# Routing 24 blocks as 6, 6, 4, 4, 4 instead of 6, 6, 5, 4, 3 in a fused attention and mixture-of-experts kernel

## The chip, the cores and the metric

The kernel runs on one core of a Trainium2 chip. The metric is device time in microseconds (us), the median of several runs. TensorE multiplies matrices, ScalarE evaluates functions and copies, VectorE and GpSimd do elementwise work, and SyncE issues most of the transfers. In the profile they are PE (PEld is TensorE's weight load), ACT, DVE, POOL and SP. An engine works through its own instructions in the order in which they are written, and waits at an instruction until what it needs from other engines has been signalled.

## The reference, cut to what matters

```
scores = scale * q @ k.T - slope_h * distance        # 4 x 8 heads, 768 tokens, head size 64
keep   = 8 global keys, and the 96 latest keys       # a window
x      = softmax(scores) @ v                         # as 3072 tokens x 512
noisy  = x @ w_gate + log1p(exp(x @ w_noise)) * noise
top2, weights = the two largest of 8 experts, softmax over the two
out[token] += weight * relu(x[token] @ w1[e]) @ w2[e]   # w1 512 x 1024, w2 1024 x 512
```

All of it is in float32. Each of the 3072 tokens goes to two of eight experts, so an expert gets about 768 tokens.

## The kernel before, in words

The 3072 tokens are 24 blocks of 128. **Attention** runs over 48 passes, two to a block, four heads to a pass (the loop variable `n` goes up by 2; the text calls n/2 the pass, from 0 to 47). In a pass VectorE makes the scores with their bias and row minimum for the next pass (`score`, L862), ScalarE takes the exponential (L865), TensorE transposes the probabilities of this pass (`trans`, L878), multiplies queries and keys for the pass after the next (`product`, L848) and probabilities with values for the pass before (`attend`, L899), and VectorE divides (`norm`, L910 to L915). `product` writes the two PSUM banks that `score` of the same pass has read, so it comes after it, and the next `score` comes after `product`. A `trans` group (L878, six transposes, four in the first block of a sequence) opens each pass on TensorE, so its start times are the passes' start times.

**The gate** of a block runs four blocks' worth of passes later, with block g in passes 2g+4 and 2g+5. `gate_t` transposes the block (L380) and copies it to SBUF (L389); `gate_l` multiplies by the gate's weights (L410) for two blocks of a routing at once, or for one where a routing's last block has no partner; `gate_s` adds up the parts (L423, L426) in the second of the two passes. `gate_l` also stores the block in DRAM: in `xd` for all blocks, in `xe` too for the blocks of the first three routings.

**Routing** turns logits into a table of which token sits at which place of which expert. It is done for a segment of blocks at a time (`SEG`), as a Python generator `route(r)` that emits one or a few instructions at each step. For a segment of w blocks it emits two ScalarE operations, some 15 small VectorE operations for log1p(exp), the top two per block (L502, L504), the weights (L527 to L539), running counts as small matmuls (L552, L554), five more small operations (L561 to L593), then for each block two masks (`mask`, L579) and one product with the masks' partner (`marks`, L603), and a group of matmuls (L628, two per block) that adds this to the table `tab` (L632). In routings 0 and 1 the blocks are marked three to a group with the masks on GpSimd. Routing 2 (`CLOSE`) has one group; where no earlier routing is still marking when it computes `row` (L585), the masks of all but two blocks go to GpSimd at once, and those two to VectorE one by one; otherwise all its masks go to GpSimd later, after L593. Routings 3 and 4 mark in groups of three, with the masks on VectorE. When routing 2 is done, GpSimd gathers the 512 first tokens of expert 0 from `xe`, and TensorE transposes them at the end of attention. Expert 0's first layer can then start on them while routings 3 and 4 are still under way.

Steps are dealt by hand-written rules. A routing starts in the pass after whose `gate_s` its last block is complete. `tick(place)` is called at seven places of a pass (0 to 3 after the four scores, 4 to 6 inside `norm`) and takes one step of one routing, routing 2 first; `finish` at the end of a pass takes three steps of routings 0 and 1 and five of the later ones. A step that yields `True` lets nothing more of that routing happen until place 4 of the next pass; one that yields 2 waits for `finish`. In the kernel before, routing 2 begins in pass 37 and routing 3 in pass 45.

**Expert 0's first layer** (`up(0, f)`, L1132) is eight units of 12 matmuls with 512 columns. After each third matmul a function `ahead` takes one of 32 entries of the table `slots`, which says how far routing 3 (`late`), routing 4 (`last`), the gate of the last block and the splitting of `w2` may go there. After each unit ScalarE takes the positive part (L1113, `hh`) and VectorE the rest that rounding left (L1117, `hl`). Splitting `w2` into a high and a low part is one ScalarE copy (L196) and one VectorE subtraction (L197) for each of eight slices. When all is done, `rank` (L301 to L315) sorts the experts by their token counts, and GpSimd gathers the other tokens. The second layer of expert 0 (`down`, L1169) follows on TensorE, and then the other seven experts, with up to 812 tokens for an expert (`CAPS`). More tokens than that would run a slow path under `tc.If` at the end.

SBUF tiles named `xg` rotate through seven buffers; `marks`, the gathers and `rank` take them in turn.

Of the kernel before, what the change touches and what calls it, by code (L numbers as in the profile page):

```python
# [10 lines left out]
F32 = mybir.dt.float32  # L11
# [10 lines left out]
P = 128  # L22
# [13 lines left out]
def tile_local_global_attention_then_moe(  # L36
# [14 lines left out]
    B, _, _, D, _, HP, Q = q.shape  # L51
    H = 2 * HP
    Dm = H * D
# [3 lines left out]
    E, _, F = w1.shape  # L57
    KC, FC = Dm // P, F // P
    NG = kT.shape[2] // NB - P
    N = B * S  # L60
    NT = B * NB
# [1 line left out]
    windowed = 1 <= n_local <= NP + 1 and 0 <= n_global <= NG  # L63
    scale = 1.0 / math.sqrt(D)
    slopes = [2.0 ** (-8.0 * (h + 1) / H) for h in range(H)]
    SEG = [(0, 6), (6, 12), (12, 17), (17, 21), (21, NT)]
    CLOSE = 2
    SW = max(z - a for a, z in SEG)

# [5 lines left out]
    gp = wctx.enter_context(tc.tile_pool(name="gp", bufs=1))  # L75
# [134 lines left out]
    xg, xt, xw = {}, {}, {}  # L210
# [163 lines left out]
    def gate_t(g):  # L374
        x = rowed[g] = XR.pop(g).rearrange("p h d -> p (h d)")
        stored[g] = gp.tile([P, 2 * Dm], U16, name="xt", bufs=4)
        halved(planes(stored[g]), words(x))
        ps = bank("m").rearrange("p (k t) -> p k t", k=KC)
        for k in range(KC):
            nc.tensor.transpose(ps[:, k], x[:, k * P:(k + 1) * P], ident)  # L380
        j = partner(g)
        if j is None:
            XT[g] = ys[2].rearrange("p (k t) -> p k t", k=KC)
            to = XT[g]
        else:
            if j == 0:
                XT[g + 1] = pairs[0].rearrange("p (k j t) -> p k j t", k=KC, j=2)
            to = XT[g + 1 - j][:, :, j]
        nc.scalar.activation(to, ps, AF.Copy)  # L389

    def store(g):
# [2 lines left out]
    def gate_l(g, later=None):  # L394
# [8 lines left out]
            return  # L403
        ps = bank("m")[:, :P]
        x = XT.pop(g)
        x = [x] if j is None else [x[:, :, i] for i in range(2)]
        for i, y in enumerate(x):
            c = 2 * E * (1 - i)
            for k in range(KC):
# [243 lines left out]
    with ExitStack() as actx:  # L653
# [142 lines left out]

        END, WAIT = 7, 8

        def begin():
            for x, _ in active:  # L800
                x.ready = {WAIT: 4, WAIT + 1: 6}.get(x.ready, 0)

        def go(y):
            x = y[0]
            v = next(x, 0)
            if v == 0:
                active.remove(y)
            elif v is True:
                x.ready = WAIT
            elif v == 2:  # L810
                x.ready = END
            elif v == LAST:
                x.ready = WAIT + 1

        def tick(place):
            for y in sorted(active, key=lambda y: y[1] != CLOSE):
                if y[0].ready <= place:
                    return go(y)

        def finish():  # L820
            for y in active[:]:
                n = 5 if y[1] >= CLOSE else 3
                while n and y in active and y[0].ready <= END:
                    go(y)
                    n -= 1

# [259 lines left out]
    with ExitStack() as mctx:  # L1086
# [118 lines left out]
        def back(e, i):  # L1205
# [11 lines left out]

        late, last = pending
        slots = {
            0: [(late, 24)], 1: [(gate_s, 2), (late, 27)], 2: [(gate_t, 1), (late, 30)], 3: [(late, 33)],  # L1220
            4: [(gate_l, 1), (late, 36)], 5: [(late, 39)], 6: [(gate_s, 1), (late, 42)], 7: [(late, 45), (last, 2)],
            8: [], 9: [(late, 48), (last, 5)], 10: [(last, 7)], 11: [(last, 8)],
            12: [(late, 52), (last, 9)], 13: [(last, 12)], 14: [(last, 14)], 15: [(late, 54), (last, 16)],
            16: [(last, 19)], 17: [(last, 21)], 18: [(last, 23)], 19: [(last, 26)],
            20: [(last, 30)], 21: [(last, 33)], 22: [(late, 57), (last, 35)], 23: [(last, 37)],
            24: [(last, 39)], 25: [(last, 42)], 26: [(late, 61)], 27: [(last, 45)],
            28: [(last, 48)], 29: [(late, 99), split], 30: [split], 31: [(last, 52)],
        }
        slot, parts = [0], [0]

# [392 lines left out]
```

## Time and profile before

| | |
|---|---|
| runs | 700.07, 835.5 and 700.47 us, median 700.47 |
| the profiled execution | 701.94 us |
| its span, first to last instruction | 700.2 us |
| mean granted TensorE clock | 0.999 |
| TensorE matmuls busy | 683.6 us, 98% |
| TensorE weight loads busy | 615.1 us, 88% |
| VectorE, ScalarE, GpSimd busy | 66%, 60%, 46% |

Attention fills the span from 0 to about 155.7 us, expert 0's first layer 155.7 to 181.1 us, and the experts the rest. Rows of the trace read as: engine, line of the kernel, operation, what is written and from what, shapes, and how many instructions were merged into the row. A time in brackets is how long the engine sat idle before it, and after the arrow stands what ended that. The profiled execution lies 1.74 us above its span and 1.47 us above the median of the runs.

### The profile page before, as it was taken

The page shows a single profiled execution, that of the slowest core. Times are in us where ns is not written, and L with a number is a line of the kernel's source. Part 1 is how long each engine was busy: PE and PEld are TensorE (multiplying, and loading weights), DVE is VectorE, ACT ScalarE, POOL GpSimd, SP SyncE. Part 2 cuts the span into 40 slices and gives each one's busy share as a digit, 9 for nine tenths or more (in the row PEclk, how much of TensorE's full clock was granted, in tenths as well). Part 3 has the DMA queues.
Part 4 walks back from the last instruction along what each step waited for, and adds up shares of the span by engine and source line. Part 5 has one row for each costly group of instructions (what it writes and reads, how often), then busy time and mean ns, then how long its engine had stood idle before and what let it go on. Part 6 is the DMA issues. An engine that isn't in the chain of part 4 may idle for free. (4 is left out here: it accounts for less than half of the span.)

```text
span 700.2 us, 16023 instructions
## 1 busy us (share of the span) xinstructions
PE 683.6 (98%) x5701; PEld 615.1 (88%) x5701; DVE 459.8 (66%) x1412; ACT 423.6 (60%) x912; POOL 324.5 (46%) x408
## 2 busy tenths in 40 slices
PE   6999999999999999999999999999999999999995
PEld 5888888888889889999999998999899899889984
DVE  7668788968928477656766676667377756757600
ACT  6888787762346576547755755486558647755510
POOL 3352837450288663264536444642645354541222
PEclk9999999999999999999999999999999999999999
DMA  8999978859394877257935884496459457842233
GB/s 249 328 306 313 277 230 282 296 168 359 116 259 91 163 181 158 49 122 136 218 60 122 166 174 75 125 168 148 82 151 249 63 136 163 184 74 91 32 47 49
DMA packets 132889, 116.61 MB, mean 167 GB/s; under 512 B 51866, under 2 KB 97050, under 8 KB 132800
## 3 DMA queue, kind: packets, MB, share of 16 engines
q1 hardware_dynamic: 121392, 89.35, 46.5%
q0 software_dynamic: 11264, 25.89, 20.3%
q8 instruction: 47, 0.77, 0.5%
q14 instruction: 42, 0.34, 0.1%
q10 hardware_dynamic: 144, 0.26, 0.1%
HBM read 71.07 MB, written 33.10 MB: 149 GB/s over the span
## 5 line engine op out<-in xcount | busy, mean ns | idle before, releaser
L1426 PE MATMUL bank<-xh,wall 128*128 128x384 f32 (+4 forms) x784 | 216.9, 342 | 1.0 <-ACT aside L1468 0.6
L1426 PEld LDWEIGHTS bank<-xh,wall 128*128 128x128 f32 x784 | 143.9, 188 | 5.4 <-ACT aside L1468 1.3
L1426 PE MATMUL bank<-xl,wall 128*128 128x384 f32 (+4 forms) x392 | 133.4, 340 | 0.0
L1145 POOL DMA_INDIRECT out_dram<-y,ids x40 | 64.7, 1617 | 124.8 <-ACT y L1142 121.0
L1169 PE MATMUL av<-w2h,hh 128*128 128x512 f32 x304 | 119.8, 394 | 1.5 <-ACT aside L1201 1.1
L197 DVE TENSOR_TENSOR wall<-raw,wall 128x512 fp32r<-128x512 f32 (+1 forms) x84 | 76.5, 918 | 66.3 <-ACT wall L196 66.2
L1169 PE MATMUL av<-w2h,hl 128*128 128x512 f32 x304 | 119.1, 392 | 0.0
L1169 PE MATMUL av<-w2l,hh 128*128 128x512 f32 x304 | 119.1, 392 | 0.0
L196 ACT ACTIVATE wall<-raw 128x512 fp32r<-128x512 f32 (+1 forms) x84 | 58.0, 698 | 47.5 <-POOL raw L1279 47.5
L1117 DVE SCALAR_TENSOR_TENSOR hl<-bank,hh 128x384 fp32r<-128x384 f32 (+4 forms) x84 | 47.1, 561 | 52.8 <-ACT hh L1113 51.8
L1426 PEld LDWEIGHTS bank<-xl,wall 128*128 128x128 f32 x392 | 73.9, 188 | 2.8
L865 ACT ACTIVATE a<-ns,mx 128x168 f32<-128x168 f32 (+1 forms) x192 | 67.8, 422 | 13.5 <-DVE mx L862 13.0
L251 POOL DMA_INDIRECT xg<-xd,ids x49 | 51.9, 1060 | 41.7 <-DVE place L302 29.8
L1169 PEld LDWEIGHTS av<-w2h,hl 128*128 128x128 f32 x304 | 57.1, 188 | 12.6
L862 DVE CUSTOM_DVE_ANT_0 ns<-sc,bias 128x168 f32<-128x168 f32 (+1 forms) x188 | 51.8, 320 | 24.3 <-PE sc L848 8.7
L1169 PEld LDWEIGHTS av<-w2h,hh 128*128 128x128 f32 x304 | 57.1, 188 | 11.0 <-ACT aside L1201 1.3
L1113 ACT ACTIVATE hh<-bank 128x384 fp32r<-128x384 f32 (+4 forms) x84 | 41.9, 498 | 39.2 <-DVE bank L1500 25.5
L1169 PEld LDWEIGHTS av<-w2l,hh 128*128 128x128 f32 x304 | 57.1, 188 | 9.4 <-DVE w2l L197 0.3
L1278 POOL TENSOR_TENSOR raw<-raw 128x256 f32<-128x256 f32 x28 | 22.1, 790 | 77.3 <-DVE wall L197 76.7
L899 PE MATMUL av<-vs,at 128*64 128x65 f32 (+1 forms) x768 | 57.3, 224 | 0.3 <-issue 0.3
L236 POOL COPY xt<-y 128x256 uint16<-128x256 uint16 x96 | 35.0, 401 | 46.7 <-DVE y L915 46.7
L899 PEld LDWEIGHTS av<-vs,at 128*64 128x64 f32 (+1 forms) x768 | 50.8, 136 | 2.4 <-issue 2.0
(219 smaller groups left out, 1465.5 us busy)
## 6 DMA issues: line engine op xcount, KB each, us to landing
raw<-in_w SPq DMA_DIRECT2D x64, 256.0 KB
raw<-in_w SPq DMA_DIRECT2D x32, 512.0 KB
out_dram<-zero SPq DMA_DIRECT2D x14, 512.0 KB
vs<-in_v SPq DMA_DIRECT2D x24, 260.0 KB
xd<-xt SPq DMA_DIRECT2D x24, 256.0 KB
qbuf<-in_q SPq DMA_DIRECT2D x23, 256.0 KB
ks<-in_k SPq DMA_DIRECT2D x20, 272.0 KB
xe<-y SPq DMA_DIRECT2D x17, 256.0 KB
```

What stands on the lines that cost most here:

```text
L196: nc.scalar.activation(hi, src, AF.Copy)
L197: eng.tensor_sub(lo, src, hi.bitcast(F32))
L236: nc.gpsimd.tensor_copy(to[:, :, c], frm[:, :, c])
L251: nc.gpsimd.indirect_dma_start(out=xg[e, t].bitcast(U16)[:m], out_offset=None, in_=xd[:n], in_offset=bass.IndirectOffsetOnAxis(ap=r, axis= ...
L862: nc.vector.tensor_tensor_reduce(out=ns[x][:, s, :w], in0=ps[:, s], in1=bias[:, u + x, s] if i else bias0[:, u + x, s], scale=-scale, scal ...
L865: nc.scalar.activation(A[n + x][:, s * w:(s + 1) * w], ns[x][:, s, :w], AF.Exp, bias=mx[x][:, s:s + 1], scale=-1.0)
L899: nc.tensor.matmul(ps[s * Q:(s + 1) * Q, h], a[r:z, part * P + q0:part * P + q0 + Q], t[r:z, c], start=k == 0 and (n == 1 or h == 0), stop ...
L1113: nc.scalar.activation(inner(e)[0][j][:, f, :src.shape[1]], src, AF.Relu)
L1117: nc.vector.scalar_tensor_tensor(lo, src, 0.0, hi.bitcast(F32), op0=OP.max, op1=OP.subtract)
L1145: ins = nc.gpsimd.indirect_dma_start(out=out, out_offset=bass.IndirectOffsetOnAxis(ap=r, axis=0), in_=y, in_offset=None, bounds_check=N + ...
L1169: nc.tensor.matmul(ps, x[j][:, f, cols], w[:, f], start=n == 0, stop=n == 3 * FC - 1)
L1426: nc.tensor.matmul(ps, wb[c % 2][u][:, 2 * a + k], x[v][:, 2 * b + k], start=start and n == 0, stop=stop and n == 5, skip_group_check=True)
```

## The change

The segments become 6, 6, 4, 4 and 4 blocks. No segment has an odd number of blocks any more, so the gate always works on pairs. The last pair, blocks 22 and 23, keeps its transposed blocks in two `xg` tiles, because its second half runs after attention's buffers are given up. A limit `PACE` is put on the steps in a pass: 99 while one of routings 0 to 2 is active, 6 while only routing 3 or 4 is. The table `slots` is written anew: routing 3 starts further along, and routing 4, a block larger, takes more steps.

```diff
-    SEG = [(0, 6), (6, 12), (12, 17), (17, 21), (21, NT)]
+    SEG = [(0, 6), (6, 12), (12, 16), (16, 20), (20, NT)]
...
@@ gate_t
-            if j == 0:
-                XT[g + 1] = pairs[0].rearrange("p (k j t) -> p k j t", k=KC, j=2)
-            to = XT[g + 1 - j][:, :, j]
+            if j == 0 and g == NT - 2:
+                XT[g + 1] = [gp.tile([P, Dm], F32, name="xg", bufs=7).rearrange("p (k t) -> p k t", k=KC) for _ in "ab"]
+            elif j == 0:
+                x = pairs[0].rearrange("p (k j t) -> p k j t", k=KC, j=2)
+                XT[g + 1] = [x[:, :, i] for i in range(2)]
+            to = XT[g + 1 - j][j]
@@ gate_l
-        x = [x] if j is None else [x[:, :, i] for i in range(2)]
+        x = [x] if j is None else x
@@ begin, go
+        PACE = (99,99,99,6,6)
+        left = [0]
         def begin():
+            left[0] = max([PACE[r] for _, r in active], default=0)
...
         def go(y):
+            left[0] -= 1
...
@@ tick, finish
-                if y[0].ready <= place:
+                if y[0].ready <= place and left[0] > 0:
...
-                while n and y in active and y[0].ready <= END:
+                while n and y in active and y[0].ready <= END and left[0] > 0:
...
         slots = {
-            0: [(late, 24)], 1: [(gate_s, 2), (late, 27)], 2: [(gate_t, 1), (late, 30)], 3: [(late, 33)],
-            4: [(gate_l, 1), (late, 36)], 5: [(late, 39)], 6: [(gate_s, 1), (late, 42)], 7: [(late, 45), (last, 2)],
-            8: [], 9: [(late, 48), (last, 5)], 10: [(last, 7)], 11: [(last, 8)],
-            12: [(late, 52), (last, 9)], 13: [(last, 12)], 14: [(last, 14)], 15: [(late, 54), (last, 16)],
-            16: [(last, 19)], 17: [(last, 21)], 18: [(last, 23)], 19: [(last, 26)],
-            20: [(last, 30)], 21: [(last, 33)], 22: [(late, 57), (last, 35)], 23: [(last, 37)],
-            24: [(last, 39)], 25: [(last, 42)], 26: [(late, 61)], 27: [(last, 45)],
-            28: [(last, 48)], 29: [(late, 99), split], 30: [split], 31: [(last, 52)],
+            0: [(late, 33)], 1: [(late, 35)], 2: [(gate_t, 1), (late, 37)], 3: [(late, 39)],
+            4: [(gate_l, 1), (late, 42)], 5: [(late, 45)], 6: [(gate_s, 1), (late, 48)], 7: [(last, 2)],
+            8: [(late, 52), (last, 5)], 9: [(last, 8)], 10: [(late, 54), (last, 10)], 11: [(last, 13)],
+            12: [(late, 57), (last, 15)], 13: [(last, 18)], 14: [(last, 21)], 15: [(late, 61), (last, 23)],
+            16: [(last, 26)], 17: [(late, 99)], 18: [(last, 30)], 19: [(last, 33)],
+            20: [(last, 36)], 21: [(last, 39)], 22: [(last, 42)], 23: [(last, 45)],
+            24: [(last, 48)], 25: [], 26: [(last, 52)], 27: [(last, 54)],
+            28: [(last, 57)], 29: [split], 30: [(last, 61), split], 31: [(last, 63)],
         }
```

For a routing of four blocks, steps 40 to 48 are the masks and marks of the first three blocks, step 52 the group's matmuls, step 54 the addition to `tab`, steps 55 to 57 the fourth block's masks and marks, step 61 its matmuls and step 63 the addition.

## Rows read from the trace of the kernel before

**Rows 1.** The page's busy times: us, share of the span, instructions.
```profile
PE 683.6 (98%) x5701; PEld 615.1 (88%) x5701; DVE 459.8 (66%) x1412; ACT 423.6 (60%) x912; POOL 324.5 (46%) x408
```

**Rows 2.** Stages: us, then busy us (instructions) of each engine, clock, DMA share, GB/s.
```profile
110.10:120.20 10.10, 9.77 (x178) 8.32 (x174) 7.08 (x40) 7.78 (x26) 8.48 (x19) 1.00 0.97 312
120.20:130.00 9.80, 9.80 (x180) 8.26 (x179) 9.26 (x69) 7.23 (x22) 1.49 (x4) 1.00 1.04 372
140.00:155.70 15.70, 15.40 (x278) 13.23 (x276) 10.10 (x49) 10.84 (x28) 8.54 (x18) 1.00 0.54 171
155.70:181.10 25.40, 25.40 (x139) 20.63 (x136) 21.41 (x105) 7.60 (x17) 0.74 (x2) 1.00 0.84 310
```

**Rows 3.** Timeline of TensorE, starts of passes 9 to 11: start us, us, instruction.
```profile
32.27 0.88 PE L878 MATMUL at<-ident,a 128*128 128x128 f32 x6
34.89 0.87 PE L878 MATMUL at<-ident,a 128*128 128x128 f32 x6
38.38 0.87 PE L878 MATMUL at<-ident,a 128*128 128x128 f32 x6
```

**Rows 4.** Timeline of TensorE, passes 37 to 44 (first row: end of pass 37).
```profile
119.45 0.88 PE L628 MATMUL lg<-xg,wall 128*128 128x168 f32 x6 [0.19 <-POOL xt L236]
120.16 0.82 PE L878 MATMUL at<-ident,a 128*128 128x128 f32 x6
121.35 0.80 PE L848 MATMUL sc<-ks,qbuf 64*64 64x168 f32 x16
122.70 0.87 PE L878 MATMUL at<-ident,a 128*128 128x128 f32 x6
135.89 1.35 PE L628 MATMUL lg<-xg,wall 128*128 128x168 f32 x10
139.65 0.88 PE L878 MATMUL at<-ident,a 128*128 128x128 f32 x6
142.89 0.64 PE L410 MATMUL m<-pair,wgn 128*32 128x128 f32 x16
```

**Rows 5.** Timeline of VectorE, passes 36 to 38.
```profile
115.26 1.43 DVE L603 TENSOR_TENSOR xg<-aside 128x336 fp32r<-128x336 f32 x3
118.78 0.33 DVE L862 CUSTOM_DVE_ANT_0 ns<-sc,bias 128x168 f32<-128x168 f32 x1 [0.27 <-PE sc L848]
121.64 0.67 DVE L488 SCALAR_TENSOR_TENSOR aside<-aside 128x40 f32<-128x40 f32 x3
```

**Rows 6.** Timeline of GpSimd, the masks of routings 1 and 2.
```profile
113.16 4.00 POOL L579 TENSOR_SCALAR wall<-iota_p,aside 128x128 fp32r<-128x128 f32 x6
131.88 4.38 POOL L579 TENSOR_SCALAR wall<-iota_p,aside 128x128 fp32r<-128x128 f32 x6 [6.47 <-DVE aside L593]
```

**Rows 7.** Timeline of VectorE in expert 0's first layer.
```profile
166.52 0.69 DVE L1117 SCALAR_TENSOR_TENSOR hl<-at,hh 128x512 fp32r<-128x512 f32 x1 [0.16 <-ACT hh L1113]
170.56 0.17 DVE L496 TENSOR_TENSOR aside<-aside,lg 128x24 f32<-128x24 f32 x1
174.25 0.48 DVE L579 TENSOR_SCALAR wall<-iota_p,aside 128x128 fp32r<-128x128 f32 x2
179.21 0.48 DVE L579 TENSOR_SCALAR wall<-iota_p,aside 128x128 fp32r<-128x128 f32 x2
179.61 0.50 DVE L603 TENSOR_TENSOR xg<-aside 128x336 fp32r<-128x336 f32 x1
182.07 3.69 DVE L197 TENSOR_TENSOR w2l<-raw,w2h 128x512 fp32r<-128x512 f32 x6
```

**Rows 8.** Timeline of TensorE in expert 0's first layer.
```profile
165.69 0.62 PE L1132 MATMUL sc<-wall,xh 128*128 128x512 f32 x2
179.83 0.61 PE L1132 MATMUL sc<-wall,xh 128*128 128x512 f32 x2
180.51 0.80 PE L628 MATMUL lg<-xg,wall 128*128 128x168 f32 x6
181.14 0.43 PE L1169 MATMUL av<-w2h,hh 128*128 128x512 f32 x1
```

## The prediction, made before the changed kernel was run

> **What bounds the kernel now.** I began with the busy times: TensorE's matmuls cover 98% of the span, VectorE's work 66% [rows 1]. That leaves 16.6 us in which TensorE shows no work, so an edit that moves other engines' work seems to have little to win. But matmuls are pipelined, and a product that waits for a bank is still shown as busy, so I looked at stages next: from 120.2 to 130.0 us VectorE is busy 9.26 of 9.80 us, and in expert 0's first layer 21.41 of 25.40 [rows 2]. In these two places VectorE's queue, in the order in which it is written, sets when TensorE may go on, and the change rewrites that order in both. Elsewhere TensorE sets the pace: passes with little routing take 2.62 us without `gate_l`'s matmuls and 3.49 with them [rows 3].
>
> **Part 1, attention.** Routing 2 is now complete after block 15, so it starts in pass 35 instead of 37, and routing 3 in pass 43 instead of 45. By the rules of `tick` and `finish` I wrote down which step falls into which pass. Before, routing 2 starts when routing 1 has marked its last three blocks: 1.43 us of `marks` in pass 36 [rows 5], table matmuls at the end of pass 37, at 119.45 [rows 4]. After, the two overlap. Routing 2 is served first at every tick, so routing 1's marks move to `finish` of passes 36 and 37 and its matmuls to the end of pass 38. By the end of pass 37 VectorE has taken in 8 small steps of routing 2 (pass 36), then 5 more, the top two of four blocks, and three small instructions (pass 37). A small step costs 0.67/3 = 0.22 us [rows 5]; 13 are 2.8 us. The rest I estimate at 1.5 us: routing 4 before, with three blocks, went from its sum L496 at 170.56 to its first mask at 174.25 with one `hl` of 0.61 us in between [rows 7], 3.1 us for about twice as many instructions. So 4.3 us are put ahead of the scores of pass 38. In passes 35 to 37 VectorE is idle 10.10 - 7.08 = 3.0 us [rows 2], but over half of that lies before this work can start; I let it take up 1.3 us. The scores start 3.0 us later than at 118.78 [rows 5], at 121.8.
>
> From there a chain of times. The four scores end at 122.8 and the product behind them at about 123.2, where before it ended at 121.35 + 0.80 = 122.15 [rows 4]. Before, pass 39 began 0.55 us after that product. After, the gate's matmuls for blocks 16 and 17 (0.64), routing 1's table matmuls (0.71, from 119.45 to 120.16) and routing 2's counts (0.2) come in between [rows 4]: pass 39 begins at 125.3 instead of 122.70. VectorE goes through 1.5 us left of pass 38 and 3.6 of pass 39 (scores 1.0, `norm` 0.6, nine small steps 2.0) and has done L593 at 127.9. There stands **a new wait**. When routing 2 computes `row` in pass 39, routing 1 is still marking, so no mask starts early and none goes to VectorE: all 8 go to GpSimd at 127.9. Six took 4.00 and 4.38 us [rows 6], so 8 take 5.3 to 5.8, and the last is there at 133.2 to 133.7. TensorE arrives at the table matmuls after pass 39 (2.6) and pass 40 (3.49 less a gate, 2.9), at about 131, and stands there until 133.5, with the transposes of pass 41 behind it, and ScalarE and VectorE waiting for those. Eight table matmuls (0.9) of this wait are work, the rest is lost. Passes 41, 42 and 43 are then undisturbed (2.62, 3.49, 2.62 [rows 3]), so pass 44 begins at 142.2 instead of 139.65 [rows 4]. In the rest of attention 0.6 us are won: the gate of a pair in the tail, as the one of 0.64 at 142.89 [rows 4], falls away. Routing 3's steps, at most six a pass, I cost at nothing: VectorE is idle 5.6 of 15.7 us from 140.0 [rows 2], and they take about 2.2; without that cover they cost 2.2. The gathers of expert 0's first tokens move two passes ahead on GpSimd with routing 2; their blocks' stores move as well, so nothing. **Sum of part 1: +2.0 us.** If VectorE's idle time takes up all 4.3 us, only the masks cost, 0.5; if it takes up none, 3.5.
>
> A product of `marks` took 0.50 us where no mask ran on GpSimd [rows 7], and three took 1.43 us where masks did [rows 5, 6]; the two engines hardly disturb each other. The Trainium skill, SBUF — State Buffer, "SBUF: two separate sides", calls the port pair that VectorE and GpSimd share an exclusive lock: a VectorE operation with two SBUF inputs and a GpSimd operation that reads SBUF fully block each other. By that rule part 1 would be dearer (rival 3); the trace does not bear it out for these two operations.
>
> **Part 2, expert 0's first layer.** Three matmuls take 180.51 - 179.83 = 0.68 us [rows 8], 32 times that is 21.8; gate, counts and table matmuls in between make the 25.4. I set VectorE's queue against TensorE's from the third unit's end, 165.69 before [rows 8]. The `hl` of that unit ends 1.44 us later (166.52 + 0.61 [rows 7]). From there to the last mark ahead of routing 4's first table matmuls (slot 26) the new `slots` put on VectorE: four blocks' masks and marks at 0.82 (179.21 to 179.61, then 0.42 [rows 7]), 3.3 us; three `hl` at 0.61, 1.8; one addition to `tab`, 0.3; and 34 small instructions, 4.6 (the 3.1 above for three blocks, 0.3 for the fourth, 1.2 for the steps ahead of and behind them). That is 10.0, so the mark is there 11.4 us after the unit's end and signalled 0.1 later. TensorE gets there after 15 thirds (10.2), two table matmuls (0.2) and the counts (0.15), at 10.6. It waits **0.9 us**. Before, at slot 31, the mark of 179.61 ended at 180.0 and the matmuls began at 180.51 [rows 7, 8]: 0.5 us to spare. The fourth block's mark now stands behind `hl` of the seventh unit, 1.44 + 0.82 = 2.26 us after that unit, and its matmuls three thirds behind, 2.04: **0.3 us** with the signal. Last, no table matmuls stand between the last unit and `down` any more (0.63, from 180.51 to 181.14 [rows 8]), so the second layer asks sooner for slices of `w2`, whose subtractions come 0.62 apart behind the last `hl` (six in 3.69 from 182.07 [rows 7]): **0.45 us**. Of TensorE's own work routing 3's counts and one `gate_s` leave (0.3), two table matmuls and half a pair's gate come (0.45). **Sum of part 2: +1.8 us**, from 0.6 (instructions 10% cheaper) to 2.6 (5% dearer, each signal 0.2).
>
> **The rest.** `rank` begins 0.3 us sooner after the last subtraction, as the addition to `tab` is done before it. It feeds the gathers that expert 0's last tokens wait for: -0.2 us. The `xg` tiles that are taken over were read well before. One store to `xe` leaves SP's queue, for which nothing waits: nothing. **Total +3.6 us**: the profiled execution's 701.94 becomes 705.5, and the median, 1.47 lower, goes from 700.47 to 704.1.
>
> **The rivals.**
> 1. *Absorbed.* VectorE's lead in passes 36 to 38 is larger than I count, and the waits at slots 26 and 30 vanish. For it: TensorE's idle time at the table matmuls of 119.45 was only 0.19 us [rows 4]. Against it: 9.26 of 9.80 us busy [rows 2]. Part 1 then gives 0 and part 2 at most 0.6: 699.5 to 701.5.
> 2. *Faster.* Routing 2 is a block shorter, so VectorE's jam in passes 39 to 43 goes. They took 139.65 - 122.70 = 16.95 us [rows 4], against 2.62, 3.49, 2.62, 2.9 and 2.62 undisturbed and 1.4 of TensorE's own counts and table: 1.3 lost. With the 0.6 of the tail and the 0.2 of `rank` that gives -2.1, 698.4; from 697.5 to 699.5. It decides at the scores of pass 38: if they start before 120.5, TensorE does not wait for them.
> 3. *Blocked.* The masks that now all run on GpSimd hold up the marks beside them: four marks, each behind one mask of 4.38/6 = 0.73 us [rows 6], 2.9 more: 707.0, from 706.6 to 709.5.
> 4. *Spill.* 16 blocks may hold other numbers of expert 0's 512 first tokens, and a token over a capacity runs the slow path: over 715. The reference's inputs give 509, and 212 more for the rest: three places stay empty, none of the 812 is overrun.
>
> **How the numbers follow.** My forecast gets 0.53, its own range 701.6 to 706.6 (+1.1 to +6.1, the bounds of both parts); rival 1 gets 0.22, rival 2 0.18, rival 3 0.05, rival 4 0.02. The range from 698.8 to 706.8 leaves out rivals 3 and 4 and over half of rival 2, about 0.18. A change is told from none at 2%, 14 us: rival 4 alone gets there, and 0.01 each way for what I have not thought of. Faster 0.01, same 0.96, slower 0.03.
>
> **What would show it.** In the changed profile: routing 1's last six table matmuls at the end of pass 38; eight masks in one run on GpSimd after L593, and eight table matmuls that wait for them; a wait of TensorE before routing 4's table matmuls. I am wrong if pass 44 begins before 140.5, or if the first layer takes under 26 us.

## The result, and the profile after

The changed kernel takes **707.36 us** (median of 6 runs, 706.52 to 711.29) against 700.27 of the kernel before on the same chip. One run of the kernel before took 835.5 us and is left out of the ratio, which is 1.0097, interval 1.0076 to 1.0117. The forecast was 704.1, its range ended at 706.8. The direction was right, the forecast loss (3.6 us) about half of the measured one (7.1), and the range was missed by 0.6 us. Its profiled execution took 708.37 us, with a span of 706.7.

Line numbers of attention's and expert 0's instructions are 3 to 8 higher than in the rows of before (the scores' L862 is L870, the table matmuls' L628 is L631).

Where the 6.5 us between the two spans lie: the first layer of expert 0 starts at 162.15 instead of 155.66 (+6.5), and lasts 27.62 instead of 25.48 (+2.1). From `down` to expert 1 it takes 0.7 less: the stretch up to the rest of expert 0's first layer is 0.2 longer, as forecast (0.45 for `w2`, less 0.2 for `rank`), and behind it the kernel before stood 1.1 us for a copy of ScalarE where the changed kernel does not, which no part of the forecast had. Most of the remaining -1.4 is one interval between two later experts (67.87 before, 66.34 after); the twelve variants of the changed kernel below have the same instructions there and show from 66.3 to 67.5, so it is probably the execution's and not the change's, but there is only one profile of before.

The stages of the changed kernel, to be read against [rows 2] (us, then busy us and instructions of PE, weight loads, VectorE, ScalarE, GpSimd, then granted clock, DMA share, GB/s). The stretches are passes 35 to 37, pass 38, passes 39 and 40, pass 43, and the first layer:

```profile
110.44:120.55 10.11, 8.75 (x159) 7.36 (x155) 7.31 (x44) 6.92 (x22) 7.76 (x19) 1.00 1.01 337
120.55:128.00 7.45, 5.70 (x73) 4.43 (x70) 5.39 (x38) 4.13 (x12) 0.54 (x1) 0.84 0.97 336
128.00:136.82 8.82, 7.73 (x131) 6.81 (x128) 6.75 (x37) 4.84 (x14) 6.75 (x12) 0.94 0.67 216
143.17:147.60 4.43, 3.02 (x60) 2.61 (x57) 1.62 (x10) 2.45 (x9) 2.54 (x6) 1.00 0.54 163
162.15:189.77 27.62, 26.39 (x145) 20.85 (x142) 21.80 (x93) 6.64 (x14) 0.81 (x2) 1.00 0.76 280
```

In the second row neither TensorE nor VectorE is near full: 5.70 and 5.39 of 7.45 us. That is not an engine that has become the bound. The engines wait for each other in turn. TensorE's timeline from pass 38 to pass 43, against [rows 4], shows where:

```profile
120.55 0.87 PE L886 MATMUL at<-ident,a 128*128 128x128 f32 x6
123.17 1.35 PE L856 MATMUL sc<-ks,qbuf 64*64 64x168 f32 x16 [1.31 <-issue]
125.48 1.01 PE L413 MATMUL m<-pair,wgn 128*32 128x128 f32 x16 [0.35 <-ACT pair L392]
126.42 1.58 PE L631 MATMUL lg<-xg,wall 128*128 128x168 f32 x6
128.00 1.34 PE L886 MATMUL at<-ident,a 128*128 128x128 f32 x6
131.18 0.88 PE L886 MATMUL at<-ident,a 128*128 128x128 f32 x6
133.50 1.20 PE L856 MATMUL sc<-ks,qbuf 64*64 64x168 f32 x13 [1.01 <-PE m L380]
135.85 1.13 PE L631 MATMUL lg<-xg,wall 128*128 128x168 f32 x8
136.82 0.83 PE L886 MATMUL at<-ident,a 128*128 128x128 f32 x6
143.17 0.87 PE L886 MATMUL at<-ident,a 128*128 128x128 f32 x6
145.45 0.41 PE L426 MATMUL lg<-sel,aside 128*128 128x32 f32 x2 [1.41 <-ACT aside L416]
147.60 0.88 PE L886 MATMUL at<-ident,a 128*128 128x128 f32 x6
```

Each L886 row opens a pass: 38 at 120.55, 39 at 128.00, 40 at 131.18, 41 at 136.82, 43 at 143.17, 44 at 147.60. Before, passes 38 and 39 opened at 120.16 and 122.70 [rows 4]. Three passes lose 8.2 us: 38 (7.46 us instead of 2.54), 40 (5.64 instead of 4.17) and 43 (4.43 instead of 2.57); others win some of it back. (Lengths are taken from unrounded starts, so the last digit may differ by one from the rows.) The gate's 16 matmuls take 1.01 us and the six table matmuls 1.58, where [rows 4] have 0.64 and 0.88 for the same work: the granted clock was at its lower level there. Of these two stretches the first lies before the fall and the second in it:

```profile
121.00:124.00 3.00, 1.60 (x18) 1.11 (x19) 2.83 (x24) 1.46 (x5) 0.09 (x1) 1.00 1.03 369
127.00:128.00 1.00, 1.00 (x10) 0.98 (x10) 0.00 (x0) 0.79 (x3) 0.00 (x0) 0.50 0.90 329
```

VectorE and GpSimd in passes 38 to 40, against [rows 5, 6]:

```profile
122.38 0.33 DVE L870 CUSTOM_DVE_ANT_0 ns<-sc,bias 128x168 f32<-128x168 f32 x1
128.18 0.19 DVE L564 TENSOR_TENSOR aside<-lg,carry 128x32 f32<-128x32 f32 x1 [2.00 <-PE lg L557]
129.74 0.16 DVE L588 SCALAR_TENSOR_TENSOR aside<-aside,sl 128x8 f32<-128x8 f32 x1
131.29 0.33 DVE L635 TENSOR_TENSOR tab<-tab,lg 128x168 f32<-128x168 f32 x1 [1.39 <-PE lg L429]
131.78 1.11 DVE L606 TENSOR_TENSOR xg<-aside 128x336 fp32r<-128x336 f32 x2
132.81 0.32 DVE L870 CUSTOM_DVE_ANT_0 ns<-sc,bias 128x168 f32<-128x168 f32 x1
```

```profile
130.07 5.39 POOL L582 TENSOR_SCALAR wall<-iota_p,aside 128x128 fp32r<-128x128 f32 x8 [8.98 <-DVE aside L588]
```

The scores of pass 38 start at 122.38 (forecast 121.8). The eight masks in one run are there, at the forecast length. One thing no step of the forecast had: the fourth row. VectorE adds routing 1's table sum (L635), which TensorE had finished at 128.0, only at 131.29, after standing 1.39 us for `gate_s` of block 17 (L429). `gate_s` writes the gate's logits, the addition reads the table sum. Both are parts of one tile, `lg`, and in the program `gate_s` stands first. The scores of pass 40 (132.81) queue behind it, and TensorE stands 1.01 us at the product of pass 40 for those. (The row names TensorE's own transposes L380, but they had ended by 132.5; in experiment 9 this wait goes together with the one of the addition.)

In the first layer the waits of TensorE are these (engine, line, waited for: us in total, times, longest):

```profile
PE lg L555 <- DVE tab L635: 0.8, 1, 0.8
PE av L1177 <- DVE w2l L197: 0.3, 1, 0.3
PE lg L631 <- DVE aside L499: 0.3, 1, 0.3
PE lg L631 <- DVE xg L606: 0.2, 1, 0.2
```

The first and the third are again two parts of `lg`: routing 4's counts (slot 18) wait until routing 3's table sum has been read, and routing 3's table matmuls (slot 15) until routing 4's logits have been read. The waits forecast for slots 26 (0.9) and 30 (0.3) are 0 and 0.2.

### The profile page after: what moved, and what is told of

The parts are those of the page before. It is cut to its first block, busy times and chain, and to the rows that moved or that the text cites. A ratio compares the mean times of both kernels' runs of the same rounds, so it can differ in the third digit from the quotient of the medians.

```text
span 706.7 us, 16009 instructions
## 1 busy us (share of the span) xinstructions
PE 684.7 (97%) x5699; PEld 615.5 (87%) x5699; DVE 459.5 (65%) x1411; ACT 423.7 (60%) x911; POOL 324.3 (46%) x410
## 4 chain that ended last, share of the span: by engine, by line
PE 79%; issue 6%; DVE 6%; ACT 3%; POOL 2%; DMA 2%; POOLq 0%; DVEq 0%; ACTq 0%
PE bank L1434 27%; PE av L1177 23%; PE av L1200 7%; PE av L907 6%; PE at L886 5%; PE sc L856 4%; PE at L1140 2%; POOL out_dram L1153 1%; PE sc L1140 1%; PE m L380 1%; PE m L413 1%; PE bank L1223 1%; PE lg L631 1%; DMA xe<-y 1%; ACT xg L282 1%
## 5 line engine op out<-in xcount | busy, mean ns | idle before, releaser
L870 DVE CUSTOM_DVE_ANT_0 ns<-sc,bias 128x168 f32<-128x168 f32 (+1 forms) x188 | 52.0, 320 | 23.7 <-PE sc L856 9.3
```

The source lines that it names most:

```text
L870: nc.vector.tensor_tensor_reduce(out=ns[x][:, s, :w], in0=ps[:, s], in1=bias[:, u + x, s] if i else bias0[:, u + x, s], scale=-scale, scal ...
```

## The experiments

My theory after the result: **A**, the overlap of routings 1 and 2 makes the loss in attention, through the order in which VectorE and TensorE wait for each other; the shared tile and a fall of TensorE's clock enlarge it. Its rivals stand in the expectations. All kernels are the changed one with the edit shown. The table gives medians, ratios to the kernel before in the same session with intervals, and from each trace the lengths of three passes, the start and length of expert 0's first layer, and for how long the clock stood at its lower level before the last experts.

| kernel | us | ratio | p38 | p40 | p43 | layer starts | lasts | lower clock |
|---|---|---|---|---|---|---|---|---|
| before | 700.27 | | 2.54 | 4.17 | 2.57 | 155.66 | 25.48 | 0 |
| after | 707.36 | 1.0097 [1.0076, 1.0117] | 7.46 | 5.64 | 4.43 | 162.15 | 27.62 | 3.4 |
| 1 two passes later | 702.66 | 1.0032 [1.0019, 1.0044] | 3.11 | 3.20 | 2.71 | 156.44 | 27.62 | 0 |
| 2 carry behind scores | 708.50 | 1.0101 [1.0076, 1.0126] | 5.59 | 3.06 | 6.72 | 161.79 | 27.63 | 6.8 |
| 3 transposes repeated | 707.78 | 1.0092 [1.0069, 1.0115] | 5.44 | 5.50 | 4.40 | 160.64 | 27.65 | 3.4 |
| 4 masks on GpSimd | 707.80 | 1.0101 [1.0075, 1.0128] | 6.38 | 5.49 | 4.38 | 160.53 | 28.01 | 0 |
| 5 two later, own bank | 701.95 | 1.0020 [1.0004, 1.0036] | 3.11 | 3.20 | 2.71 | 157.26 | 26.67 | 3.4 |
| 6 routing 1 first | 705.48 | 1.0061 [1.0036, 1.0086] | 5.17 | 4.15 | 2.76 | 159.11 | 27.61 | 6.8 |
| 7 segment's gate last | 706.90 | 1.0086 [1.0061, 1.0112] | 7.51 | 5.46 | 2.86 | 161.02 | 27.64 | 3.4 |
| 8 one pass later | 702.76 | 1.0034 [1.0019, 1.0048] | 5.25 | 3.03 | 2.76 | 156.21 | 27.65 | 0 |
| 9 gate behind steps | 705.75 | 1.0076 [1.0055, 1.0097] | 7.51 | 4.02 | 2.76 | 159.98 | 27.60 | 6.8 |
| 10 four masks on VectorE | 706.27 | 1.0081 [1.0056, 1.0106] | 5.34 | 5.49 | 2.76 | 160.05 | 27.61 | 3.4 |
| 11 both 9 and 10 | 704.97 | 1.0066 [1.0044, 1.0087] | 6.39 | 4.45 | 2.76 | 157.77 | 27.61 | 0 |
| 12 one later, own bank, no limit | 702.92 | 1.0036 [1.0022, 1.0050] | 5.25 | 3.03 | 2.76 | 157.17 | 26.70 | 0 |

**1. Routing 2 appended two passes later** (where the kernel before starts it).

```diff
-                            active.append((Steps(route(ends.index(g))), ends.index(g)))
+                            if ends.index(g) != CLOSE:
+                                active.append((Steps(route(ends.index(g))), ends.index(g)))
+                        if g == ends[CLOSE] + 1:
+                            active.append((Steps(route(CLOSE)), CLOSE))
```

> The changed kernel, but routing 2 (blocks 12 to 15) starts in pass 37 as before, two passes after it could. Theory A (the overlap of routings 1 and 2 puts VectorE's queue behind in passes 36 to 40): the 6.8 us lost between the starts of passes 38 and 41 are gone, pass 44 starts between 139.0 and 141.5 instead of 147.6, and the time falls from 707.0 to 700.5 to 703. Rival B (routing 3's earlier start in pass 43 and the limit PACE cost the time): routing 3 still starts in pass 43, so pass 44 may recover but the end of attention does not, and the time stays above 705.

Attention's loss falls from 6.5 to 0.8 us (first layer at 156.44) and the ratio from 1.0097 to 1.0032, while the first layer keeps its 27.62. Attention's loss is the overlap and what follows from it, and nearly nothing else.

**2. The wait at the counts behind the scores** (in `route`, ahead of the first instruction that reads the counts).

```diff
             yield from weigh()
+            yield True
         nc.vector.tensor_add(po, pos, carry[:, None, :].to_broadcast(sh))
```

> The changed kernel, but routing 2's addition of the counts to the carry (L564) waits for place 4 of a pass instead of being taken between the third and the fourth score. Theory A1 (in pass 39 VectorE stood 2.0 us at that addition, with the fourth score behind it, because the counts' matmuls stand at the end of TensorE's pass 38): that idle time goes, passes 39 and 40 lose 1 to 2 us, the time becomes 705.0 to 706.2. Rival A2 (TensorE is late anyway from pass 38 on, so what VectorE does not wait for here it waits for at the next score): 706.6 to 707.6.

VectorE no longer stands 2.0 us at L564, and pass 40 shrinks to 3.06. The time does not fall: 708.50 lies above both ranges, so the run does not decide between them. Pass 43 takes 6.72. ScalarE waits 4.05 us at its copy L416 there, and TensorE's `gate_s` for that copy. In after the copy and what it reads are these (timeline of TensorE and ScalarE):

```profile
142.59 0.64 PE L413 MATMUL m<-pair,wgn 128*32 128x128 f32 x16
145.12 0.28 ACT L416 ACTIVATE aside<-m 128x128 f32<-128x128 f32 x1 [2.58 <-PE at L886]
```

The copy reads what L413 writes, whose records end at 143.23, but it starts 1.9 us later, and its releaser is TensorE: the signal came late. Experiments 3 and 4 show the same lateness (1.8 each), and here it is 2.7, with a releaser that the profile does not name; in all the others the copy starts 0.07 us behind the matmuls. What held the signal I could not read from the traces, and it stays open.

**3. The gate's transposes of block 17 three times** (so that TensorE works where it stood).

```diff
-        for k in range(KC):
+        for k in range(KC * (3 if g == 17 else 1)):
+            k %= KC
             nc.tensor.transpose(ps[:, k], x[:, k * P:(k + 1) * P], ident)
```

> The changed kernel, but the gate's four transposes of block 17 in pass 38 are issued three times into the same bank (same data), 8 more of about 0.13 us, in the 1.3 us for which TensorE stood idle ahead of that pass's product. Theory C (after that idle stretch the granted clock fell to half from 125.6 to 129.0 us, which cost about 1.7 us in that execution): no half-speed stretch in attention, pass 39 starts 1.0 to 1.3 us earlier than 128.0, and the time is 705.5 to 706.5. Rival: the fall is not tied to that idle stretch, or is in few executions: time 706.5 to 707.6 and a half-speed stretch still there.

Inconclusive: in this execution the clock fell at 119.3, ahead of the added work. The time, 707.78, shows no gain, against theory C's 705.5 to 706.5.

**4. All masks of routings 3 and 4 on GpSimd.**

```diff
+        if r > CLOSE:
+            for i in range(w):
+                mask(i, nc.gpsimd)
         yield
```

> The changed kernel, but the masks of routings 3 and 4 are made by GpSimd, all four blocks' as soon as row (L588) is there, and no longer by VectorE. Theory D (in expert 0's first layer VectorE's queue is what TensorE waits for): 16 masks less, 0.39 us a pair, so 3.1 us less on VectorE; the waits at slots 15, 18, 26 and 30 (1.4 us in sum) go, the first layer takes 25.9 to 26.6 us instead of 27.6, and the time is 705.3 to 706.2. Rival E (the table's PSUM tile, not the masks, makes the counts wait): the 0.80 us at slot 18 stays and the layer takes 27 us or more.

VectorE's busy time in the first layer fell from 21.80 to 19.25 us, and the layer became longer, not shorter: 28.01. The 0.8 us at slot 18 stayed, as rival E had it, and TensorE now waited 0.5 us for masks of GpSimd. VectorE's load is not what the first layer waits for; theory D fell. This run gave something else. Up to pass 42 its instructions are those of after, and its clock did not fall (stages, as above):

```profile
127.00:128.00 1.00, 1.00 (x12) 0.83 (x14) 0.91 (x7) 0.59 (x3) 0.00 (x0) 1.00 0.96 318
```

and its timeline in passes 38 to 40 has these rows:

```profile
123.11 1.34 PE L859 MATMUL sc<-ks,qbuf 64*64 64x168 f32 x16 [1.31 <-issue]
126.00 0.90 PE L634 MATMUL lg<-xg,wall 128*128 128x168 f32 x6
128.95 5.42 POOL L582 TENSOR_SCALAR wall<-iota_p,aside 128x128 fp32r<-128x128 f32 x8 [7.92 <-DVE aside L588]
129.86 0.33 DVE L638 TENSOR_TENSOR tab<-tab,lg 128x168 f32<-128x168 f32 x1 [1.08 <-PE lg L429]
131.92 1.20 PE L859 MATMUL sc<-ks,qbuf 64*64 64x168 f32 x13 [0.86 <-PE m L380]
134.27 1.13 PE L634 MATMUL lg<-xg,wall 128*128 128x168 f32 x8
135.24 0.83 PE L889 MATMUL at<-ident,a 128*128 128x128 f32 x6
```

Its first layer starts at 160.53, so in after's execution the fall cost about 162.15 - 160.53 = 1.6 us, and attention's loss without it is 4.9. The wait for the shared tile is there as well. The forecast wait for the masks is not: the eight table matmuls start at 134.27, 0.1 us before the last mask ends (134.37), show no idle time, and pass 41 opens 0.97 us later. After has the same 0.97 (135.85 to 136.82), with its masks done at 135.46. The masks stand close behind, though: pass 40 is 1.5 us shorter in experiment 9, without the tile's wait, and by that estimate TensorE would come to the table matmuls before the masks end. Experiments 9 to 11 look at the two.

**5. Experiment 1, with the counts of routing 4 in a bank of their own.**

```diff
-        ps = lgp
+        ps = bank("m") if r == len(SEG) - 1 else lgp
```

> The kernel after with routing 2 appended two passes later (702.7 us by itself, first layer 27.62 us), and the counts of routing 4 written into a PSUM bank of their own instead of the bank that they share with routing 3's table sums. Theory F, the shared bank: in the first layer TensorE's 0.80 us at the counts of slot 18 is a wait for VectorE's addition to tab, which reads another part of the same bank; without it the first layer takes 26.8 to 27.0 us and the whole 701.8 to 702.1. Rival G, the prediction's own picture: VectorE's queue sets slot 26 anyway, so what is saved at slot 18 comes back at slots 26 and 30; the first layer takes 27.4 us or more, and the whole 702.4 to 702.9.

```profile
173.31 0.19 PE L555 MATMUL m<-aside,upper 128*128 128x32 bf16 x1
```

The counts have no wait any more, and the first layer takes 26.67 instead of 27.62: **theory F**, the shared tile, to within 0.15 us. What was saved did not come back at slots 26 and 30, so the prediction's picture, that VectorE's queue sets slot 26, is refuted. The whole, 701.95, is where F had it.

**6. The older routing served first.**

```diff
-            for y in sorted(active, key=lambda y: y[1] != CLOSE):
+            for y in active[:]:
```

> The kernel after, with the older routing served first at every step instead of routing 2 first. Theory H, the order of service: routing 1's last marks and table matmuls are back in pass 37 and fewer of routing 2's steps stand ahead of the scores of pass 38; pass 38 takes under 4.0 us (after: 7.46, or 6.38 where the clock did not fall), the first layer starts at 157 to 159, and the whole takes 703.5 to 705.5 us. Rival I, the amount of work: both routings' steps lie in passes 36 to 42 whatever their order, so the wait moves to later passes; the first layer starts at 160 or later, and the whole takes 706.5 us or more.

The whole, 705.48, is at the upper end of H, but pass 38 keeps 5.17 us where H wanted under 4.0, and pass 37 grows to 6.86, with 6.8 us at the lower clock in these two. The order of service may be a part of the loss, not all; how large a part, the fall of the clock hides.

**7. `gate_s` of a segment's last block behind `attend`.**

```diff
-                        if g in ends:
+                        if False:
...
+                if g >= 0 and odd and g in ends:
+                    gate_s(g)
+                    active.append((Steps(route(ends.index(g))), ends.index(g)))
```

> The kernel after, with the gate_s of a segment's last block (passes 11, 23, 35, 43) issued behind attend instead of ahead of the next product, so that TensorE does not stand at it for ScalarE's copy (1.41 us in pass 43). Theory J: pass 43 takes 3.0 to 3.3 us instead of 4.4, the first layer starts 1.1 to 1.4 us earlier (159.1 to 159.5 where the clock does not fall), and the whole takes 705.9 to 706.4 us. Rival K: the copy stands behind the exponentials in ScalarE's queue and TensorE's next transposes wait for the same exponentials, so passes 44 and 45 take it back; the first layer starts within 0.4 us of 160.5 and the whole takes 707.0 us or more.

Undecided between J and K. Pass 43 shrinks by 1.6 us, but in this execution ScalarE's copy was on time, so the edit did not meet the wait that it was to pass by. It moves the start of every routing and costs 0.7 earlier (pass 34 opens at 107.60 instead of 106.94). The whole lies between the two theories and is not told from after's.

**8. Routing 2 one pass later.**

```diff
                     else:
+                        if g == ends[CLOSE] + 1:
+                            active.append((Steps(route(CLOSE)), CLOSE))
                         gate_t(g)
```

> The kernel after with routing 2 appended one pass later (pass 36), half of the delay that brought the time down to 702.7 us. Theory A, overlap: what is lost grows with the steps of routing 2 that stand ahead of routing 1's end; with one pass less of overlap the first layer starts at 157.5 to 159 and the whole takes 703.7 to 705.5 us. Rival L, a threshold: either the jam is all there as soon as the two routings meet (first layer at 160 or later, 706.5 us or more), or one pass is enough to be rid of it (first layer before 157, under 703.2 us).

A threshold (**L**): first layer at 156.21, as good as two passes. Pass 38 is still 5.25 long, so the jam at its scores is largely there. But routing 1's table sum is added before `gate_s` of block 17 comes, and as routing 1 has then marked all, only four masks go to GpSimd; passes 40, 42 and 45 give back what pass 38 lost:

```profile
125.74 0.30 DVE L635 TENSOR_TENSOR tab<-tab,lg 128x168 f32<-128x168 f32 x1
132.12 0.62 DVE L582 TENSOR_SCALAR wall<-iota_p,aside 128x128 fp32r<-128x128 f32 x2
```

**9. `gate_s` inside a segment written behind `finish`.** All engines' instructions stay the same and in the same order; only which access to `lg` counts as earlier changes.

```diff
-                if g >= 0 and odd and g not in ends:
-                    gate_s(g, True)
...
                     finish()
+                if g >= 0 and odd and g not in ends:
+                    gate_s(g, True)
```

> The kernel after, with gate_s of the blocks inside a segment written behind finish instead of ahead of it. Every engine's instructions and their order stay as they are; only the order in which accesses to the shared tile lg count changes, so that routing 1's last addition to tab no longer waits for gate_s of block 17, which writes another part of that tile. Theory M, the shared tile decides in pass 40: VectorE's wait of 1.1 to 1.4 us there vanishes, the scores of pass 40 start about 1 us sooner, TensorE's wait of 0.9 to 1.0 us at the next product vanishes, and pass 40 shrinks from 5.5 to 4.5 to 4.9 us (the eight masks on GpSimd then set its end); the whole takes 0.5 to 1.0 us less than after, 706.4 to 706.9. Rival N, the masks alone set pass 40: VectorE's wait goes, the eight masks still run 5.4 us from the same instant, pass 40 keeps 5.3 us or more, and the whole stays at 707.1 us or more.

```profile
129.71 0.15 DVE L588 SCALAR_TENSOR_TENSOR aside<-aside,sl 128x8 f32<-128x8 f32 x1
129.78 0.32 DVE L635 TENSOR_TENSOR tab<-tab,lg 128x168 f32<-128x168 f32 x1
130.03 5.26 POOL L582 TENSOR_SCALAR wall<-iota_p,aside 128x128 fp32r<-128x128 f32 x8 [9.04 <-DVE aside L588]
135.52 1.13 PE L631 MATMUL lg<-xg,wall 128*128 128x168 f32 x8
136.48 0.82 PE L886 MATMUL at<-ident,a 128*128 128x128 f32 x6
```

The addition follows at once, TensorE's wait at the product of pass 40 is gone, and pass 40 takes 4.02 us: **M**'s mechanism is shown, and N's 5.3 us or more fell. The whole, 705.75, is below M's range. But what the edit is worth at the full clock this execution does not tell. It had the lower clock until 131.6, pass 39 took 4.49 us (2.86 in experiment 4), and from `row` (L588), which starts the masks, to pass 41 it takes 129.71 to 136.48, 6.77 us, in experiment 4 128.62 to 135.24, 6.62. The masks do not set that end: they are done at 135.29, TensorE comes to the table matmuls at 135.52, and pass 41 opens 0.96 us later. Whether they would have set it with TensorE 1.6 us earlier is not shown. In this profile pass 43 is shorter too, 2.76 us instead of 4.4.

**10. Four of routing 2's masks on VectorE.**

```diff
-        if r == CLOSE and not marking:
+        if r == CLOSE:
```

> The kernel after, with routing 2's masks dealt as if routing 1 were done: four on GpSimd as soon as row is there, four on VectorE between the marks (0.31 us each). Theory N, the masks set pass 40 as the prediction said: pass 40 shrinks from 5.5 to under 4.7 us, the whole to 706.5 us or less. Theory M, the shared tile: VectorE still stands for gate_s, the scores of pass 40 come no sooner, TensorE still waits 0.9 us at the product, and the four masks add 1.2 us to VectorE; pass 40 keeps 5.0 us or more and the whole 707.0 us or more.

```profile
131.18 0.33 DVE L635 TENSOR_TENSOR tab<-tab,lg 128x168 f32<-128x168 f32 x1 [1.09 <-PE lg L429]
133.23 1.20 PE L856 MATMUL sc<-ks,qbuf 64*64 64x168 f32 x13 [0.86 <-PE m L380]
135.58 1.13 PE L631 MATMUL lg<-xg,wall 128*128 128x168 f32 x8
```

VectorE and TensorE stand for the shared tile as before, pass 40 keeps 5.49 us, and from `row` to pass 41 it is 129.93 to 136.55, 6.62 us: as **M** had it, fewer masks on GpSimd alone win nothing here. GpSimd's four masks end at 133.01, 2.6 us ahead of the table matmuls, and those still come no sooner. The whole, 706.27, is in N's range; in this profile pass 43's late signal is gone too.

**11. Both.** (The edits of 9 and 10.)

> The kernel after with both edits: gate_s behind finish, and four of routing 2's masks on VectorE. If the shared tile and the masks limit pass 40 side by side, the two together give more than the sum of each: pass 40 takes 3.9 to 4.4 us, passes 39 to 41 together 9.7 to 10.0 us as in the kernel with routing 2 one pass later (9.71) instead of 10.9, and the whole 705.8 to 706.4 us. If it is the one or the other alone, this run equals the better of the two within 0.3 us.

```profile
128.65 0.16 DVE L588 SCALAR_TENSOR_TENSOR aside<-aside,sl 128x8 f32<-128x8 f32 x1
134.22 0.82 PE L886 MATMUL at<-ident,a 128*128 128x128 f32 x6
```

From `row` to pass 41 it is 5.57 us now, 1.05 less than in experiments 4 and 10. With four masks on VectorE, then, doing away with the shared tile's wait is worth 1.05 us. Passes 39 to 41 take 9.92 us (126.91 to 136.83), as expected, and pass 40 4.45, just over the expected 4.4. That it takes both edits is not shown: the masks' edit alone wins nothing (experiment 10), but the tile's alone was run only with a fall of the clock in that very stretch (experiment 9). The whole, 704.97, is below the expected 705.8; in this profile pass 43's wait no longer stands.

**12. Experiment 8 with the bank of experiment 5 and no limit of steps.** (`begin` sets `left[0] = 99`.)

> The kernel after with routing 2 one pass later (702.8 us by itself, first layer 27.65 us), the counts of routing 4 in a bank of their own (worth 0.95 us of first layer where it was tried) and no limit on the steps of a pass. Theory O, the limit of six steps a pass leaves work of routing 3 to the first layer, where VectorE is short, and its zero in the first pass of routing 0 costs 0.3 us: the first layer takes 25.6 to 26.2 us, attention 0.3 us less, and the whole 700.3 to 701.2 us. Rival P, the slots set the pace of the first layer whatever was done before it, or the steps moved forward jam passes 43 to 47: the first layer takes 26.5 us or more, or starts after 156.6, and the whole takes 701.5 us or more.

**O** fell, and **P** holds: the first layer keeps 26.70 with more of routing 3 done before it, and starts at 157.17, as pass 46 gets longer (4.36 us, in experiment 8 3.33). No version tried is faster than the kernel before; the nearest is experiment 5, 0.2% behind it.

## Why the prediction was wrong, point by point

**Part 1, the chain of times, is the step that failed** (+2.0 forecast; +4.9 at the full clock, +6.5 in the profiled execution). Its wait for the masks did not come; what came in its place and beside it were the wait for a shared tile, a late signal in pass 43 and, in the profiled execution, the lower clock. Starts of the first layer, at the full clock but for the last, give the parts as differences of single profiles:

- Before to experiment 8, 155.66 to 156.21: +0.55. All of the change but the second pass of overlap costs this.
- Experiment 8 to 11, 156.21 to 157.77: +1.6. The second pass of overlap, with the shared tile and the masks out of the way: the scores of pass 38. The step was seen. Its 3.0 us of lateness came out at 3.6 (122.38), and in experiment 4 pass 39 opened at 126.88 instead of the forecast 125.3, as the product behind the scores ended at 124.45 instead of 123.2 and the gate's matmuls then stood 0.35 us for ScalarE.
- Experiment 11 to 4, 157.77 to 160.53: +2.8. The shared tile in pass 40, with the masks dealt anew too (1.05), and 1.6 of the late signal in pass 43 (4.38 against 2.76), the cause of which is open. The forecast had neither; it had a wait for the masks. "Passes 41, 42 and 43 are then undisturbed" was the wrong sentence: they take 10.75 us in experiment 4 instead of 8.73.
- Experiment 4 to after, 160.53 to 162.15: +1.6. TensorE's clock, in the profiled execution. The forecast took every TensorE row at the full clock. The median does not hold this part (see the last section).

From pass 39 to pass 41 the forecast had 8.2 us (125.3 to 133.5), and experiment 4 has 8.36. That agreement is luck. The eight masks ran as forecast, but TensorE did not wait for them; it came late to the table matmuls, held in pass 40 by the scores behind the shared tile. After pass 44 the forecast won 0.6 us, the runs won 1.5 (14.54 us to the first layer in experiment 4, 16.01 before [rows 4]). So Part 1's terms missed by +1.6 (pass 38), +0.2 (passes 39 and 40, where one wait stood in for another), +2.0 (passes 41 to 43), -0.9 and, for the clock, +1.6; together +4.5, which is 6.5 less the 2.0.

Why did the forecast not see the shared tile? I set VectorE's queue against TensorE's by what each instruction computes. But the waits go by tile, and `gate_s` and `route` use one tile `lg` for logits, counts and table sums. The rows of before name `lg` for table sums and logits [rows 4, 7]; I did not ask who else writes it. The Trainium skill, "PSUM — Partial Sum Buffer", section "PSUM bank collisions raise a hardware error", says that two engines must be kept apart on one bank and quadrant (32 partitions) even where they touch different columns, and the rows above have `lg` over all 128 partitions. So such a wait can't simply be dropped; a kernel can change the order (experiment 9) or the bank (experiment 5). No run here shows a collision.

**Part 2 was near in its sum** (+1.8 forecast; +2.1 in the layer and +0.2 from `down` to the rest of the layer) **and wrong in its place, so the sum is luck.** VectorE's queue had room: slots 26 and 30 waited 0 and 0.2 us instead of 0.9 and 0.3. Instead, 0.8 and 0.3 went to the shared tile at slots 18 and 15; experiment 5, which lifts the first, gave back 0.95. TensorE's wait for `w2l` in `down`, forecast as 0.45, is 0.3 by the waits above, and 0.5 by the time from the first matmul of `down` to the ninth (2.51 us, before 2.01). Of the 1.2 us that the layer of experiment 5 is still longer than before, its waits show 0.5; the rest I did not take apart.

**The rivals.** Absorbed and faster: the scores of pass 38 started at 122.38, not before 120.5, and attention neither kept its time nor won. But the gain that "faster" counted is real: experiment 8 has pass 40 at 3.03 (before 4.17) and pass 45 at 2.62 (before 3.56). In after it was spent by pass 38, pass 40 and pass 43. Blocked: two marks beside masks took 1.11 us, 0.55 each, against 0.50 alone [rows 7]. So the rule of the Trainium skill, "SBUF — State Buffer", section "SBUF: two separate sides", by which such a pair would block each other for whole instructions, is not what this trace shows. Spill: no.

**The signs to look for.** Routing 1's six table matmuls at the end of pass 38, and eight masks in one run: there. Eight table matmuls that wait for the masks: not there. In after they start at 135.85, after the last mask's end at 135.46, and in experiment 4 at 134.27 without a wait. A wait ahead of routing 4's table matmuls: 0 at slot 26, 0.2 at slot 30. I had named bounds below which I would be wrong, and none above: pass 44 at 147.6 was beyond anything in my range.

## What to carry to other kernels

Where two pipelines of work are made to overlap, list for each wait the tile, not the value: who else writes or reads any part of it, and which of them comes first in the program. A summed chain of times along one engine is a lower bound when two engines wait for each other in turn; and TensorE's clock may add to it. That two engines' work ends at nearly the same time does not show that one waits for the other: look whether the waiting engine's row has idle time, and whether what follows it comes later than where the other work was done early (experiments 4, 9 and 10). Limits that may hide each other are to be tested singly and together, from the event that starts both, and at the same clock: one fall of it left the single test of experiment 9 open.

## What the runs showed of the hardware

TensorE's granted clock went to half (from its level of 2.4 to that of 1.2 GHz) within attention after a stretch in which it partly stood: 1.60 busy us of 3.00 from 121.0 in after, and then 3.4 us at the lower level. It did so in seven of the twelve experiments' profiles too, for 3.4 or 6.8 us in all, and not in experiment 4, whose stretch from 121 to 124 has practically the same busy time (1.61). So the same instructions may or may not pay, 1.6 us here; a difference of that size between two profiles says nothing before the clock has been looked at. The mean granted clocks of after's six runs are 0.995 (the profiled one), 0.997, 0.998, 0.998, 0.993 and 0.998. Every profile without a fall in attention has 0.997 or more, every one with a fall 0.996 or less, so after's median, 707.36, is one of executions without a fall: the clock is a part of the profiled loss, and not of the median's. The other surprise is the late signal of TensorE in pass 43 (1.9 us behind its matmuls' records; 0.07 in experiment 9, which has the same instructions), whose cause stays open.
